# Attention rows scattered straight to expert order, K and V of the dense steps in quarters, logits in 64-column tiles

## The chip, the cores and the metric

The kernel runs on one core of a Trainium2 chip. The metric is the device time of one launch in microseconds (us). A profiled execution also has a span, from its first to its last instruction.

## What is computed

Sparse attention over 4 batches, 8 heads, 768 positions and 64 numbers a head, and then a layer of 8 experts of which each of the 3072 tokens uses one:

```python
scores = scale * np.matmul(q, k.transpose(0, 1, 3, 2))
mask = np.abs(blk_i - blk_j) <= 1                  # blocks of 32
mask |= (blk_i == 0) | (blk_j == 0) | (blk_i == 23) | (blk_j == 23)
# and three sampled key blocks for every query block
attn = softmax(np.where(mask, scores, -1e9)); x = attn @ v
x = x.transpose(0, 2, 1, 3).reshape(3072, 512)
logits = x @ w_gate; e_idx = argmax(logits)
gate_w = softmax(logits)[e_idx]; eom = sigmoid(x @ w_output_gate)
for e in range(8):
    m = e_idx == e
    out[m] = gate_w[m] * eom[m, e] * (np.maximum(x[m] @ w1[e], 0) @ w2[e])
```

## The kernel before

**Attention** runs in 52 steps, 26 for each of two batch pairs (`bp`). The first four of a pair are dense (the first and last query block see all keys; `u` numbers the step, each takes two heads of both batches), the other 22 are sparse: 11 pairs of query blocks (`i`), each in two steps (`hg`). A step's stages are spread over three turns of the loop at L1125: turn n computes scores of unit n (`pS`, L454 and L523), the O product of unit n-2 (`pO`, L488 and L554) and the transposes of unit n-1 (`pT`). Around them `at(step, rank, f, ...)` hangs loads, copies and routing (L970 to L1055). The order of each engine's instructions is the order of the program (`in_order`, L80), and a load that is `paced` (L93) waits for the last TensorE instruction ahead of it.

K of a batch pair is one tile `kn`, 3.1 MB, V of the dense steps one tile `vn`, 3.1 MB; the first pair loads them at the start (L980 to L984), K in two halves and then V in six parts; the second pair's come in twelve loads at steps 8 to 24 (L999 to L1001). For a sparse pair the kernel copies K blocks into a ring `kr` on GpSimd (`gather_k`, L384, and `fixed`) and VectorE (`window_k`, L401), and gathers V rows from device memory with two indirect DMAs on GpSimd's queue (`gather_v`, L411), 128 rows of 4160 B each, into a ring `vt` of three.

**Routing.** Each 128 finished tokens (a tile, 24 in all) go to device memory as `xscr` (`store_x`, L578, two stores on SyncE's queue), are transposed (`turn`, L585), and give 16 logits by four fp32 matmuls (`route_p`, L603), which the trace shows as eight passes. In groups of tiles (`RG`, L45) VectorE works out expert, gate and the place of each token in expert order (`route_a`, L614, and `route_c`, L661); `route_d` (L695) scatters rows of 16 B (output index, row in `xscr`, gate) into the DRAM tensor `table`. `plan_ops` (L712) then makes the list of expert units: units 0 and 1 are tiles of experts 0 and 1 that are started before routing ends; 15 further ones (and a conditional rest) are single tiles or pairs.

**Expert part.** `program` (L1062) lays it out in steps, eight to a unit, one for each 128 of the 1024 hidden numbers. For unit u, whose first step is t = 8u: `load_t` (t-18) fetches its part of the table on SyncE's queue, `load_x` (t-9) gathers its x rows by it on GpSimd's queue, `x_s` (t-7) splits x in two halves of fp16 (ScalarE, VectorE), `x_t` (t-5) transposes it, for units from 4 on by DMA transposes on SyncE's queue. `piece_load` (L1059) loads the 512 KB weight pieces on SyncE's queue into a ring of 16, only when the expert changes; `w_h` and `w_l` split them (ScalarE, VectorE); `p_h` and `p_y` are the matmuls, `h_h` and `h_l` the ReLU halves `hh`; `y_o` scales, `store_y` (t+13) writes by an indirect DMA on GpSimd's queue; the second store of a pair waits for the first to land. The buffers of `tab` are four: `load_t` of unit u needs that of u-4, which `store_y` frees. The plan stands at step 6 (`PLAN`, L63).

The lines on which steps of the prediction rest:

```python
src = table[ds(row[0], 128 * m)].rearrange("(p m) c -> p m c", m=m)   # L814, load_t
after_scatters(nc.sync.dma_start(tabs[u][:, 0:m], src).ins)
nc.gpsimd.indirect_dma_start(                                         # L841, load_x
    xfs[u][:, m], None, src, bass.IndirectOffsetOnAxis(ap=tabs[u][:, m, 1:2], axis=0))
nc.tensor.matmul(lp[:, 0:16], x[:, c], wst[:, c], start=c == 0, stop=c == 3)   # L607
```

Of the kernel before, what the change touches and what calls it, by code (L numbers as in the profile page):

```python
# [27 lines left out]
NROW = EMPTY + 1024  # L28

# [15 lines left out]
RG = ((0, 4), (4, 8), (8, 12), (12, 16), (16, 19), (19, 24))  # L45
GT = max(b - a for a, b in RG)

GE = 3
# [14 lines left out]
PLAN = 6, (40,)  # L63
# [9 lines left out]
PARTS = (5, 5, 4), (5, 5)  # L73
# [35 lines left out]
def tile_kernel(ctx, tc, q, k, v, sampled, wg, wcat, out):  # L109
# [15 lines left out]
    xscr = dram.tile([NTOK, DM], F32, name="xscr")  # L125

    table = dram.tile([NROW, 4], I32, name="table")

# [15 lines left out]
    lim = const.tile([1, NE], F32, name="lim")  # L144
    base8 = const.tile([128, 8], F16, name="base8")
    tile8 = const.tile([PS, 8], I32, name="tile8")
    tilef = const.tile([PS, 8], F32, name="tilef")
    vals = const.tile([128, NT, 4], I32, name="vals")
# [36 lines left out]
    wi = sp.tile([128, NPAIR, 2], I32, name="wi")  # L185
    wf = sp.tile([128, NPAIR, 2], F32, name="wf")
    dup = sp.tile([128, NB, 3], F32, name="dup")

    def setup_iota():
# [13 lines left out]
        nc.gpsimd.iota(vals[:, :, 1], pattern=[[128, NT]], base=0, channel_multiplier=1)  # L203
        nc.gpsimd.memset(vals[:, :, 3], 0)
# [16 lines left out]
    def setup_const():  # L221
# [8 lines left out]
        nc.vector.tensor_scalar(lim, iota128[0:1, 0:NE], float(LS), 128.0, op0=ALU.mult, op1=ALU.add)  # L230

# [6 lines left out]
    def setup_vals():  # L238
# [5 lines left out]

        nc.gpsimd.memset(places, 0)
# [21 lines left out]
    def setup_index():  # L267
# [19 lines left out]
        nc.vector.tensor_copy(vals[:, :, 0], vf.rearrange("p a b -> p (a b)"))  # L287
# [41 lines left out]
    def setup_rest():  # L329

        tz = stg.tile([128, 1024], F32, tag="stg", name="tz").bitcast(I32)[:, 0:NROW // 32].rearrange("p (n c) -> p n c", c=4)
        nc.gpsimd.memset(tz, 0)
        nc.gpsimd.memset(tz[:, :, 0:1], 2 * NTOK)
        nc.sync.dma_start(table.rearrange("(p n) c -> p n c", p=128), tz)


    ntt = NT
# [6 lines left out]
    kr = [ring.tile([128, 12, 256], F32, name=f"kr{i}") for i in range(RK)]  # L344
# [4 lines left out]
    kn, vn = {}, {}  # L349

    def prep_alloc(bp):
        kn[bp] = big.tile([128, NB, 256], F32, tag="kn", name=f"kn{bp}", bufs=2)

    def prep_alloc_v(bp):
        vn[bp] = big.tile([128, 6, 2, 8, VW], F32, tag="vn", name=f"vn{bp}", bufs=1)

    def load_k(bp, c):
        nc.sync.dma_start(kn[bp][:, c], k[bp, :, c])

    def load_v(bp, c):  # L360
        nc.sync.dma_start(vn[bp][:, c].rearrange("p b j w -> p (b j w)"), v[769 * bp + 128 * c:769 * bp + 128 * c + 128])
# [10 lines left out]

    def fixed(bp, r):
        for j in range(2):
            nc.gpsimd.tensor_tensor(
                kr[r][:, 10 + j], kn[bp][:, 23 * j], eighth.to_broadcast([128, 256]), op=ALU.mult)
# [7 lines left out]
    def gather_k(bp, i, kind, ns):  # L384
# [5 lines left out]
        for n, rv in zip(ns, regs):  # L390
            slot = n + 4 if n < 3 else n - 2
            if kind == "dve":
                nc.vector.tensor_single_scalar(r[:, slot:slot + 1], kn[bp][:, ds(rv, 1)], EXPS, op=ALU.mult)
            elif kind == "act":
                nc.scalar.activation(r[:, slot:slot + 1], kn[bp][:, ds(rv, 1)], AF.Copy, scale=EXPS)
            else:
                nc.gpsimd.tensor_tensor(  # L397
                    r[:, slot], kn[bp][:, ds(rv, 1)].rearrange("p o n -> p (o n)"), eighth.to_broadcast([128, 256]),
                    op=ALU.mult)

    def window_k(bp, i):  # L401
        a = 1 + 2 * i
        r = kr[i % RK]
        nc.vector.tensor_single_scalar(r[:, 0], kn[bp][:, a + 2], EXPS, op=ALU.mult)
        nc.vector.tensor_single_scalar(r[:, 7:10], kn[bp][:, a - 1:a + 2], EXPS, op=ALU.mult)
# [13 lines left out]
    xt = {}  # L419

    def new_x(bp, i):
        if (bp, i) not in xt:
            xt[bp, i] = att.tile([128, 2, 4, D], F32, tag="x", name=f"x{bp}_{i}", bufs=3)
        return xt[bp, i]
# [787 lines left out]
```

## Time and profile before

| | |
|---|---|
| median of three runs | 628.8 us (625.73 to 629.6) |
| profiled execution | 631.68 us |
| its span | 629.9 us |
| its mean granted TensorE clock | 0.951 |
| busy share of the span: TensorE, its weight loads, VectorE, ScalarE, GpSimd | 88%, 62%, 63%, 53%, 37% |

A line of a timeline has start and length in us, the engine, the source line, operation, output and inputs, the count of merged instructions, and in brackets the idle time before it and what ended it. PE is TensorE, PEld its weight loads, DVE VectorE, ACT ScalarE, POOL GpSimd, SPq the queue of SyncE. A wait is put down to what came last by the profile and can be another one.

### The profile page before, as it was taken

Reading aid. Unit: us, or ns where it says so; the run is one execution under the profiler, and the core shown is the slowest. Engines: PE = TensorE matmul, PEld = TensorE weight load, DVE = VectorE, ACT = ScalarE, POOL = GpSimd, SP = SyncE. Lnnn points to the kernel's source line nnn. Section 1 sums busy time; section 2 is a strip of 40 time slices with the busy share of each in tenths; the row PEclk is TensorE's granted clock in tenths of the full one; section 3 lists DMA queues with packets and bytes.
Section 4 is the critical chain, followed back from the end, with each engine's and each line's share of the span. In section 5 each row is a group of like instructions: output and inputs, shape, how many; then the busy total and the mean of one; then the engine's idle time right before and its main releaser. Section 6 shows DMA issues by size and latency. Waiting matters only on the chain. (4 is left out here: it accounts for less than half of the span.)

```text
span 629.9 us, 18639 instructions
## 1 busy us (share of the span) xinstructions
PE 553.2 (88%) x7234; PEld 390.7 (62%) x7234; DVE 396.1 (63%) x741; ACT 335.2 (53%) x584; POOL 230.6 (37%) x317
## 2 busy tenths in 40 slices
PE   4788998798898899878699987999969999799993
PEld 3366776575676676656466655666646666566662
DVE  3468676554684666847967575656656566585560
ACT  1445565455465456555467574555744556465550
POOL 4256666736266656541421203122122203222021
PEclk7698999989999999899799999999988999899997
DMA  8747999984599998664294299962947617667962
GB/s 316 212 106 219 284 304 276 240 242 80 136 237 317 291 288 242 136 185 107 79 400 164 71 284 303 333 154 52 271 147 221 187 34 252 168 201 225 298 247 105
DMA packets 68796, 132.53 MB, mean 210 GB/s; under 512 B 32479, under 2 KB 38751, under 8 KB 68448
## 3 DMA queue, kind: packets, MB, share of 16 engines
q1 hardware_dynamic: 56960, 93.65, 49.3%
q0 software_dynamic: 11744, 37.64, 20.6%
q8 instruction: 59, 0.97, 0.6%
q14 instruction: 33, 0.27, 0.1%
HBM read 137.58 MB, written 14.12 MB: 241 GB/s over the span
## 5 line engine op out<-in xcount | busy, mean ns | idle before, releaser
L910 PEld LDWEIGHTS <-kr 128*128 128x128 f16 x1200 | 105.7, 100 | 52.6 <-issue 22.8
L895 DVE SCALAR_TENSOR_TENSOR kr<-r,kr 128x1024 f16<-128x1024 f32 (+1 forms) x104 | 119.9, 1179 | 23.5 <-ACT kr L891 18.5
L910 PE MATMUL h<-xb,kr 128*128 128x256 f16 (+1 forms) x1080 | 121.3, 263 | 13.7 <-DVE hh L925 7.1
L941 PE MATMUL y<-kr,hh 128*128 128x512 f16 x501 | 127.3, 385 | 0.0
L955 POOL DMA_INDIRECT out_dram<-yo,tab x28 | 32.7, 1168 | 237.7 <-ACT yo L949 181.1
L891 ACT ACTIVATE kr<-r 128x1024 f16<-128x1024 f32 (+1 forms) x104 | 102.4, 1018 | 0.8 <-DMA r<-in_wcat_dram 0.5
L941 PEld LDWEIGHTS <-hh 128*128 128x128 f16 x672 | 64.9, 99 | 52.2 <-issue 3.0
L397 POOL TENSOR_TENSOR kr<-kn,eighth 128x256 f32<-128x256 f32 x132 | 77.8, 618 | 16.2 <-issue 15.9
L919 ACT ACTIVATE hh<-h 128x512 f16<-128x512 f32 (+1 forms) x68 | 35.2, 518 | 89.6 <-PE h L910 85.3
L414 POOL DMA_INDIRECT vt<-in_v_dram,vidx x44 | 43.6, 992 | 82.6 <-PE O L508 41.9
L472 DVE TENSOR_REDUCE mx<-S 128x4 f32<-128x1024 f32 x44 | 53.7, 1221 | 28.6 <-PE S L465 20.5
L480 ACT ACTIVATE P<-S,mx 128x256 f32<-128x256 f32 x176 | 69.5, 488 | 3.1 <-DVE mx L472 2.3
L925 DVE SCALAR_TENSOR_TENSOR hh<-h,hh 128x512 f16<-128x512 f32 (+1 forms) x68 | 40.4, 594 | 48.7 <-ACT hh L919 48.7
L433 ACT COPY pt<-T 128x512 f32<-128x512 f32 x66 | 37.0, 590 | 43.1 <-PE T L430 36.1
L465 PE MATMUL S<-kr,qall 64*32 64x256 f32 x1408 | 53.0, 402 | 1.0 <-issue 0.8
L895 DVE SCALAR_TENSOR_TENSOR ws<-r,ws 128x1024 f16<-128x1024 f32 (+1 forms) x39 | 44.1, 1146 | 14.6 <-ACT ws L891 14.6
L430 PE MATMUL T<-ident,P 128*128 128x128 f32 x352 | 50.4, 289 | 0.1
L508 PE MATMUL O<-vt,pt 128*32 128x65 f32 x1408 | 34.4, 225 | 12.9 <-DMA vt<-in_v_dram,vidx 11.0
L910 PEld LDWEIGHTS <-ws 128*128 128x128 f16 x432 | 35.8, 98 | 14.0 <-ACT kr L891 2.4
L941 PE MATMUL y<-ws,hh 128*128 128x512 f16 x171 | 43.8, 388 | 0.0
L430 PEld LDWEIGHTS T<-ident,P 128*128 128x128 f32 x352 | 41.7, 148 | 2.4 <-issue 0.4
L910 PE MATMUL h<-xb,ws 128*128 128x256 f16 (+1 forms) x360 | 38.4, 256 | 3.4 <-DMA xb<-xb 1.9
(233 smaller groups left out, 689.9 us busy)
## 6 DMA issues: line engine op xcount, KB each, us to landing
r<-in_wcat_dram SPq DMA_DIRECT2D x152, 512.0 KB
vn<-in_v_dram SPq DMA_DIRECT2D x12, 520.0 KB
qall<-in_q_dram SPq DMA_DIRECT2D x24, 256.0 KB
xscr<-x SPq DMA_DIRECT2D x48, 128.0 KB
vc<-in_v_dram SPq DMA_DIRECT2D x22, 260.0 KB
kn<-in_k_dram SPq DMA_DIRECT2D x2, 1536.0 KB
kn<-in_k_dram SPq DMA_DIRECT2D x6, 512.0 KB
vc<-in_v_dram SPq DMA_DIRECT2D x12, 130.0 KB
```

The lines of the kernel that those rows point to most:

```text
L397: nc.gpsimd.tensor_tensor(r[:, slot], kn[bp][:, ds(rv, 1)].rearrange("p o n -> p (o n)"), eighth.to_broadcast([128, 256]), op=ALU.mult)
L414: nc.gpsimd.indirect_dma_start(vt[bp, i][:, s].rearrange("p b j w -> p (b j w)"), None, v, bass.IndirectOffsetOnAxis(ap=vidx[:, bp, i, s:s ...
L430: nc.tensor.transpose(pt[:, 128 * c:128 * c + 128], p[:, 128 * c:128 * c + 128], ident)
L433: nc.scalar.copy(t[:, 0:w], pt[:, 0:w])
L465: nc.tensor.matmul(s[64 * h2 + 32 * qi:64 * h2 + 32 * qi + 32, b, hp], t[p, 64 * j + 32 * qi:64 * j + 32 * qi + 32], g[p, 1 - qi:3:1 + qi, ...
L472: nc.vector.tensor_reduce(mx, self.s.rearrange("p b h n -> p (b h) n"), axis=AX.X, op=ALU.max, negate=True)
L480: nc.scalar.activation(p[:, 256 * hp:256 * hp + 256], self.s[:, b, hp], AF.Exp, bias=self.mx[:, 2 * b + hp:2 * b + hp + 1])
L891: nc.scalar.activation(w[:, 0, r], piece(n // 8, n % 8)[:, r], AF.Copy, scale=SW)
L895: nc.vector.scalar_tensor_tensor(w[:, 1, r], piece(n // 8, n % 8)[:, r], SW, w[:, 0, r], op0=ALU.mult, op1=ALU.subtract)
L910: nc.tensor.matmul(hps[n // 2][:, cols(n)], w[:, hl, 128 * c:128 * c + 128], x[:, xl, c], start=cnt == 0, stop=cnt == 11)
L925: nc.vector.scalar_tensor_tensor(hl[:, k], hps.pop(g)[:, k], 0.0, hh[:, k], op0=ALU.max, op1=ALU.subtract)
L941: nc.tensor.matmul(y, a[:, k], w[:, l, 512:1024], start=n % 8 == 0 and cnt == 0, stop=n % 8 == 7 and cnt == 2)
```

## The change

K is laid out by dense step (`u`): a quarter of 786 KB each, and `kr`, the score matmuls and the copies take 64-number runs. The halves of an array that held the two batches of a pair now hold two halves of the heads, so that a token's 512 numbers of x lie in one partition. V of the dense steps is a second copy in device memory in the order of the steps, four loads of 799 KB into the ring `vt`; for the second pair they stand at steps 23, 25, 27 and 28. `vn` is gone. `xscr` and `table` are gone: x lies in a ring `xall` of 8 tiles whose rows have 16 more places, for output index and gate; `route_d` scatters these rows of 2112 B to `rows`, in expert order. The first four routing groups have three tiles instead of the first three of four. The plan works out place indices (`place_u`) of each unit's rows, `load_x` gathers `rows` by them, and `keep_t` copies index and gate out of the gathered rows on GpSimd. `load_t` only reads registers. Ten weight pieces instead of twelve are loaded early, six instead of four at the end of attention.

The core of the diff:

```diff
-RG = ((0, 4), (4, 8), (8, 12), (12, 16), (16, 19), (19, 24))
+RG = ((0, 3), (3, 6), (6, 9), (9, 12), (12, 16), (16, 19), (19, 24))
...
-PLAN = 6, (40,)
+PLAN = 6, (60,)
...
-    def load_k(bp, c):
-        nc.sync.dma_start(kn[bp][:, c], k[bp, :, c])
...
+    def load_k(bp, u, c):
+        nc.sync.dma_start(kn[bp][:, u, c], k[bp, u, :, c])
...
+    def load_v(bp, u):
+        t = ring.tile([128, 2, 2, 8, VW], F32, tag="vt", name=f"vq{bp}_{u}", bufs=RV)
+        t = t.rearrange("p a b j w -> p (a b j w)")[:, 0:VQ]
+        nc.sync.dma_start(t, vdense[4 * bp + u])
...
-    def store_x(bp, i, tt):
-        rows = xscr[128 * tt:128 * tt + 128]
...
+        nc.gpsimd.tensor_copy(x[:, DM:DM + 1], vals[:, tt:tt + 1])
...
         for c in range(4):
-            nc.tensor.matmul(lp[:, 0:16], x[:, c], wst[:, c], start=c == 0, stop=c == 3)
+            for h in range(2):
+                nc.tensor.matmul(
+                    lp[64 * h:64 * h + 64, 0:16], x[:, c, 64 * h:64 * h + 64], wst[:, c], start=c == 0, stop=c == 3)
...
     def route_d(t):
         i = nc.gpsimd.indirect_dma_start(
-            table, bass.IndirectOffsetOnAxis(ap=place[:, t:t + 1], axis=0), vals[:, t], None).ins
+            rows, bass.IndirectOffsetOnAxis(ap=place[:, t:t + 1], axis=0), x_of(t).bitcast(I32), None).ins
...
+        ends = sp.tile([PS, 17], F32, tag="bad", name="ends")
+        yield nc.vector.tensor_copy(ends[:, 0:16].rearrange("p (t e) -> p t e", t=2), cp[0:PS, 0:8].unsqueeze(1).to_broadcast([PS, 2, 8]))
+        yield nc.vector.memset(ends[:, 16:17], 0.0)
+        yield nc.vector.tensor_tensor(ee[:, 1], own[:, 0], ends, op=ALU.mult)
...
+        lb = bank("lb", True)
+        nc.tensor.matmul(lb[:, 0:2 * PS], ones[0:PS], left.rearrange("p a b -> p (a b)"), start=True, stop=True)
...
+        yield nc.vector.tensor_single_scalar(place_u[:, NE:], lu, float(EMPTY), op=ALU.add)
...
     def load_t(u):
         m = tiles_of(u)
-        tabs[u] = rt.tile([128, 2, 4], I32, tag="tab", name=f"tab{u}", bufs=4)
...
-        after_scatters(nc.sync.dma_start(tabs[u][:, 0:m], src).ins)
...
+    def keep_t(u):
...
+        nc.gpsimd.tensor_copy(tabs[u][0][:, 0:m], xfs[u][:, :, DM])
+        nc.gpsimd.tensor_copy(tabs[u][1][:, 0:m], xfs[u][:, :, DM + 1])
...
-            nc.gpsimd.indirect_dma_start(
-                xfs[u][:, m], None, src, bass.IndirectOffsetOnAxis(ap=tabs[u][:, m, 1:2], axis=0))
+            after_scatters(nc.gpsimd.indirect_dma_start(
+                xfs[u][:, m].bitcast(I32), None, rows, bass.IndirectOffsetOnAxis(ap=place_u[:, u, m:m + 1], axis=0)).ins)
...
-    load_k(0, slice(0, 12))
-    load_k(0, slice(12, 24))
-    scale_q(0, NPAIR)
-    for c in range(6):
-        load_v(0, c)
+    for u in range(3):
+        load_k(0, u, slice(0, NB))
+        load_v(0, u)
+        if u == 0:
+            scale_q(0, NPAIR)
+    load_k(0, 3, slice(0, NB))
...
+    at(2, 1, load_v, 0, 3)
...
-    for c in range(6):
-        at(8 + 3 * c, 3, load_k, 1, slice(4 * c, 4 * c + 4))
-        at(9 + 3 * c, 3, load_v, 1, c)
+    for c in range(8):
+        at(8 + 2 * c, 3, load_k, 1, c // 2, slice(12 * (c % 2), 12 * (c % 2) + 12))
+    for u in range(4):
+        at(PER + (-3, -1, 1, 2)[u], 1, load_v, 1, u)
...
-            at(r, 3, store_x, bp, i, tt)
...
-    for j in range(8 * NE):
-        at((PER + ND + 1 + j, PER + ND + 1 + j, NSTEP - 3 + (j - 12))[j // 6], 3, prefetch_w, j)
+    for j in range(NRAW):
+        at(PER + ND + 1 + j if j < NRAW - 6 else NSTEP - 3 + (j - NRAW + 6), 3, prefetch_w, j)
...
+            do(t + 1, 13, keep_t, u)
```

## Rows read from the trace of the kernel before

**Rows 1.** The page: the span in 40 slices of 15.75 us.

```profile
PEclk7698999989999999899799999999988999899997
DMA  8747999984599998664294299962947617667962
GB/s 316 212 106 219 284 304 276 240 242 80 136 237 317 291 288 242 136 185 107 79 400 164 71 284 303 333 154 52 271 147 221 187 34 252 168 201 225 298 247 105
```

**Rows 2.** Waits: engine, line waited for; us in total, times, longest.

```profile
PE h L910 <- DVE hh L925: 13.3, 4, 4.7
...
PE O L508 <- DMA vt<-in_v_dram,vidx: 11.0, 9, 2.6
...
PE h L910 <- DMA xb<-xb: 7.2, 3, 2.9
```

**Rows 3.** Timeline of the first 16 us, VectorE and TensorE.

```profile
10.22 0.47 DVE L327 CAST vidx<-tab 128x22 int32<-128x22 f32 x1
...
13.73 0.90 PE L532 MATMUL S0d<-kn,qall 64*64 64x384 f32 x1 [2.14 <-DMA kn<-in_k_dram]
...
15.34 0.96 DVE L540 TENSOR_REDUCE mx0d<-S0d 128x1 f32<-128x768 f32 x1 [4.65 <-PE S1d L532]
```

**Rows 4.** Timeline of TensorE in a sparse step with logits.

```profile
88.58 1.09 PE L465 MATMUL S<-kr,qall 64*32 64x256 f32 x32
89.61 1.06 PE L607 MATMUL lp<-wst,xT 128*128 128x16 f32 x8
90.60 0.69 PE L497 MATMUL O<-vc,pt 128*64 128x65 f32 x16
91.22 0.67 PE L508 MATMUL O<-vt,pt 128*32 128x65 f32 x32
...
92.83 1.09 PE L465 MATMUL S<-kr,qall 64*32 64x256 f32 x32
```

**Rows 5.** The page: DMA issues, count and KB of each.

```profile
r<-in_wcat_dram SPq DMA_DIRECT2D x152, 512.0 KB
vn<-in_v_dram SPq DMA_DIRECT2D x12, 520.0 KB
...
xscr<-x SPq DMA_DIRECT2D x48, 128.0 KB
...
kn<-in_k_dram SPq DMA_DIRECT2D x6, 512.0 KB
```

**Rows 6.** Timeline: a V gather on GpSimd's queue, and TensorE.

```profile
95.88 0.97 POOL L414 DMA_INDIRECT vt<-in_v_dram,vidx  x1 [0.52 <-PE O L508]
...
104.88 0.66 PE L508 MATMUL O<-vt,pt 128*32 128x65 f32 x30 [1.72 <-DMA vt<-in_v_dram,vidx]
```

**Rows 7.** Waits of SyncE's queue.

```profile
SPq L815 <- DMA out_dram<-yo,tab: 55.3, 9, 8.0
...
SPq L806 <- DMA table<-vals,place: 9.6, 2, 5.7
```

**Rows 8.** Timeline of GpSimd late in attention: the first x gather.

```profile
268.88 0.98 POOL L841 DMA_INDIRECT xf<-xscr,tab  x1 [5.75 <-DMA vc<-in_v_dram]
270.16 1.43 POOL L414 DMA_INDIRECT vt<-in_v_dram,vidx  x1 [0.30 <-issue]
```

**Rows 9.** Timeline of the plan: VectorE's first and last instruction, and TensorE.

```profile
299.86 0.15 DVE L717 TENSOR_SCALAR ci<-cp 19x8 int32<-19x8 f32 x1
...
305.07 0.14 DVE L773 CAST es<-most 19x1 int32<-19x1 f32 x1
...
306.85 1.44 PE L910 MATMUL h<-xs,kr 128*128 128x128 f16 x12 [4.73 <-DVE hh L925]
```

**Rows 10.** Timeline of one round of expert units.

```profile
441.50 9.21 SPq L820 DMA_DIRECT2D r<-in_wcat_dram  x6
...
450.80 4.43 SPq L865 DMA_TRANSPOSE xb<-xb  x2
...
458.65 1.47 PE L910 MATMUL h<-xb,ws 128*128 128x256 f16 x12 [1.91 <-DMA xb<-xb]
...
466.26 1.06 ACT L851 ACTIVATE xb<-xb 128x1024 f16<-128x1024 f32 x1 [8.21 <-issue]
...
470.36 2.72 PE L910 MATMUL h<-xb,kr 128*128 128x256 f16 x12 [3.72 <-DVE hh L925]
```

More of the change, by code (lines that the diff above doesn't have):

```diff
@@ L27 @@
 EMPTY = E * LS
-NROW = EMPTY + 1024
+NROW = EMPTY + 1
+XP = DM + 16
+VQ = 6 * 2 * 2 * 65
+VGAT = 2 * (S + 1)
+NX = 8
+NRAW = 16
+OOB = 4096
 NE = 2
@@ L122, in tile_kernel @@
     psO = actx.enter_context(tc.tile_pool(name="psO", bufs=2, space=PSUM))
-    xscr = dram.tile([NTOK, DM], F32, name="xscr")
-    table = dram.tile([NROW, 4], I32, name="table")
+    rows = dram.tile([NROW, XP], I32, name="rows")
     ident = const.tile([128, 128], F32, name="ident")
@@ L144, in tile_kernel @@
     lim = const.tile([1, NE], F32, name="lim")
+    early = const.tile([128, NE], F32, name="early")
+    rowid = const.tile([128, PS, 2], F32, name="rowid")
+    place_u = const.tile([128, NE + PS, 2], I32, name="place_u")
     base8 = const.tile([128, 8], F16, name="base8")
@@ L230, in setup_const @@
         nc.vector.tensor_scalar(lim, iota128[0:1, 0:NE], float(LS), 128.0, op0=ALU.mult, op1=ALU.add)
+        nc.vector.tensor_scalar(early, iota128[:, 0:NE], float(LS), pcol[:, 0:1], op0=ALU.mult, op1=ALU.add)
+        nc.vector.tensor_copy(rowid, rid)
         nc.vector.tensor_scalar(tri, iota128, pcol[:, 0:1], None, op0=ALU.is_gt)
@@ L329, in setup_rest @@
     def setup_rest():
[L331 to L337, printed above, removed]
+        nc.gpsimd.memset(xall[0:1, NX - 1, 0:DM], 0.0)
+        nc.gpsimd.memset(xall[0:1, NX - 1, DM:DM + 1], float(OOB))
+        nc.sync.dma_start(rows[EMPTY:EMPTY + 1], xall[0:1, NX - 1].bitcast(I32))
     oh = const.tile([128, NT, 8], F16, name="oh")
@@ L527, in pS @@
             for half in range(2):
[L528 to L531 removed]
+                for b in range(2):
+                    for h2 in range(2):
+                        j = 2 * u + b
+                        p = slice(64 * h2, 64 * h2 + 64)
                         nc.tensor.matmul(
[L533 to L534 removed]
+                            self.s[h2][64 * b:64 * b + 64, half, 0:384], t[p, 64 * j:64 * j + 64],
+                            kn[bp][p, u, 12 * half:12 * half + 12, 32 * b:32 * b + 32], start=True, stop=True)
         def dM(self):
@@ L546, in aE @@
                 for half in range(2):
[L547 removed]
+                    p = att.tile([128, XP], F32, tag="P", name=f"P{b}{half}" + self.name, bufs=6)
                     nc.scalar.activation(p[:, 0:384], self.s[b][:, half, 0:384], AF.Exp, bias=self.mx[b])
@@ L668, in route_c @@
             yield nc.vector.scalar_tensor_tensor(c0, lack, 0.0, c0, op0=ALU.max, op1=ALU.add)
+            over = rt.tile([128, NE], F32, name="over")
+            yield nc.vector.tensor_tensor(over, early, rp[:, 256:256 + NE], op=ALU.is_lt)
+            yield nc.vector.scalar_tensor_tensor(over, early, float(-EMPTY), over, op0=ALU.add, op1=ALU.mult)
+            yield nc.vector.tensor_single_scalar(place_u[:, 0:NE, 0], over, float(EMPTY), op=ALU.add)
         t0, t1 = RG[g]
@@ L827, in xring @@
             for i in range(3):
-                t = ring.tile([128, 2, 1024], F32, tag="vt", name=f"xb{i}", bufs=RV)
-                xbuf.extend(t[:, c] for c in range(2))
-        return xbuf[n]
+                t = ring.tile([128, 2 * (DM + XP)], F32, tag="vt", name=f"xb{i}", bufs=RV)
+                xbuf.append(t)
+        return xbuf[n % 2 if n < 4 else 2][:, (slice(0, 2 * XP), slice(2 * XP, 2 * XP + 1024), slice(1024 * (n % 2), 1024 * (n % 2) + 1024))[n // 2]]
     def load_x(u):
@@ L1087, in program @@
             if n >= 8 * NE:
-                do(max(n - 16 - LEAD + 1, end), 14, piece_load, n, n1 + ahead)
+                do(max(n - NRAW - LEAD + 1, end), 14, piece_load, n, n1 + ahead)
+            elif n >= NRAW:
+                do(n - NRAW - LEAD + 1, 14, prefetch_w, n)
             do(PH.get(n, n), 8, p_h, n)
```

232 lines of the change are left out of this document (119 added, 113 removed).

## Prediction

> **What bounds the kernel now.** I read the page's slices first, then the waits, then the timeline of four places: the start, a sparse step, the join of attention and experts, and one round of expert units. The slices [rows 1] are 15.75 us each. The first 18 or so are attention, the rest the expert part; the DMA engines are at 0.9 or more in slices 5 to 8 and 12 to 15, at 237 to 317 GB/s, and in the expert part they swing between 0.1 and 0.9. TensorE (PE) is the engine that the end hangs on. In a sparse step without waits [rows 4] it works without a gap: S at 88.58, logits at 89.61, O at 90.60, the next S at 92.83, so 4.25 us of which the logits hold 0.99. What PE waits for is in [rows 2]: 11.0 us for gathered V in nine waits, 13.3 us on `hh` and 7.2 us on transposed x in the expert part. After a long wait the same work also runs slower: 12 matmuls that took 1.47 us at 458.65 took 2.72 us at 470.36, after 3.72 us idle [rows 10]. So a wait that goes gives back more than its own length.
>
> **The change part by part.** My sum is made against the profiled execution: span 629.9 us, 631.7 us in all. The median of the runs shown, 628.8, is 2.9 lower; I subtract the same saving from both.
>
> *Start.* The first dense step needed all of K (3.1 MB, two loads); its second half let PE start at 13.73, and the first reduction ran at 15.34 [rows 3]. Now it needs a quarter, 786 KB, which is half of the 1.57 MB of the first old load, so it should land near 6 to 7 us. Next in line is VectorE: its setup ends at 10.69 (10.22 plus 0.47 [rows 3]), and the two setup instructions added stand ahead of its wait for the sampled blocks. The reduction then starts at 10.7: 4.6 us earlier. Low end 0, if a later quarter is late (the four quarters of K and three of V go out alternately, 5.5 MB before the last); high end 7, if PE also leaves its slow clock sooner. I take 4.6. The K copies for the first sparse step, on GpSimd (POOL) and VectorE, now wait for the fourth quarter; the four dense steps before that step cover them.
>
> *Logits.* Per tile of 128 tokens, 8 passes with 128 weight columns took 0.99 us (89.61 to 90.60). The new form is 16 passes with 64 columns; the nearest row is the O product, 16 passes of 128*64 in about 0.62 us [rows 4]. So 0.37 us a tile, 24 tiles, 8.9 us at most, and only where PE and not a transfer sets the step. The low end is a loss: twice the passes at the old 0.12 us each, 23.8 us more. It is nearest to the O row, which has the same tile form, so I take the gain, at half the tiles: 4.5 us.
>
> *K and V loads of the second batch pair.* Before, every three steps of the first sparse run brought 512 KB of K and 520 KB of V [rows 5], 0.69 MB for the two steps of a block pair. Now 393 KB of K per pair; V comes as four 799 KB loads around the second dense run, where slice 10 shows the DMA engines at 0.4 [rows 1]. That is 0.3 MB less per pair, 1 us at 290 GB/s, over eight pairs with full queues. The gather at 95.88 needed until 104.88 to serve PE, which lost 1.72 us [rows 6]. Bounds: 0 if gathers stay late, 11.0 [rows 2] plus the slow work behind. I take 5. Two of the twelve early weight pieces (512 KB each [rows 5]) also move to the end of attention; 3.6 us of transfer out of full slices; I take 1 of 0 to 3.6.
>
> *x rows.* The 48 stores of 128 KB [rows 5] go from SyncE's (SP's) queue; 24 scatters of 128 rows x 2112 B (270 KB) replace 24 of 16 B rows in POOL's queue. The count and the issue time on POOL stay, the bytes on the engines too (6.3 against 6.5 MB). Added are one copy of a column per tile and two per unit on POOL; between gathers POOL has idle time before its wait on PE (0.5 us at 95.88 [rows 6]) and that covers them; uncovered, at the 0.15 us of VectorE's shortest instructions [rows 9], 24 of them would be 3.6 us. The K copies read four runs of 64 numbers instead of 256 in a row; the same idle time covers a step's copies unless they grow by 0.5 us together. The V gathers now queue behind scatters: see the second rival. A seventh routing group puts some twenty short VectorE instructions more under PE's steps, nothing on the path.
>
> *No table.* POOL stood 5.75 us at 268.88 before its first x gather, with the V gathers of the last pairs behind it [rows 8]; the profile names a V load, but SP waited 9.6 us twice in all for the scatters of the table before it could fetch it [rows 7], and the gather needs that table. Now the gather waits for its scatters alone, issued a step earlier. I take 2.5 us of 0 to 5.75 for PE. In the expert part SP's table load had to wait for a free table buffer, that is for an old store of the output: 55.3 us in nine waits, up to 8.0 [rows 7], with weight loads behind it in SP's queue. At 441.50 six came in a row, and the transposes of x at 450.80, behind them in the same queue, served PE only at 458.65 (wait 1.91); the store and the x gather came late in turn, ScalarE stood 8.21 us until 466.26, and PE 3.72 us until 470.36 [rows 10]. Without the table, loads start up to 8 us earlier, in time when the DMA engines idle (0.2 and 0.1 in slices 28 and 33 [rows 1]). At stake: 7.2 plus 13.3 less 4.73 (the plan, below), 15.8 us, and some 6 us of slow work behind three such rounds (an estimate: two blocks a round, 1.25 us longer each, 2.72 less 1.47, with a lighter round among them): 0 to 22. The store, not the table, stays ahead of the x gather on POOL, so I take a third: 7.
>
> *Plan.* VectorE's plan ran from 299.86 to 305.21, and PE stood 4.73 us for the `hh` behind it [rows 9]. Eleven short instructions (0.15 us like the rows, plus gaps) and one matmul go in: 2.2 us. The matmul stands in PE's queue right behind the plan's first, so PE now waits before, not after, some 2.7 us of expert work, and does that work once the plan lets it go. Loss between 1.5 and 5; I take 2.5.
>
> Sum: 4.6 + 4.5 + 5 + 1 + 2.5 + 7 - 2.5 = 22.1 us. 631.7 - 22.1 = 609.6 for a profiled execution, 628.8 - 22.1 = 606.7 for the median: **607 us**.
>
> **Rivals.**
> (a) *The expert part gives nothing* (SP's wait was slack: six loads in a row still end before the weights are used, and the x gather stays behind the store): 15.1 us remain, 614. For it: no wait of weight in [rows 2]; against it: the queue order at 450.80.
> (b) *The scatters hold up the V gathers*: slower. Nineteen scatters have a gather queued behind them. At 95.88 a gather of 532 KB took 8 us from its issue's end to PE [rows 6]; a scatter of half the bytes would add up to 4 us, if full. With 2 us each, 38 us: 628.8 + 38 - 22 = 645. It decides from 22.1 / 19 = 1.2 us each. Against it: the same bytes went over the same engines before, and the relief in K and V is as large. The Trainium skill ("DMA: Bandwidth & Descriptors", "Queues, rings and completion order") has each DMA engine take turns between queue rows; by it the gathers and scatters would now share POOL's turn, while SP's queue keeps its own. No row here shows the turns.
> (c) *The narrow logits cost double*, since each moves only 16 columns: 23.8 lost instead of 4.5 won, 628.8 - 17.6 + 23.8 = 635. The Trainium skill ("TensorEngine Tiling (Array Packing)", "Performance Considerations") warns of this: a small matmul has a fixed overhead, so tiling should not be taken from a dimension that is small already. The O row speaks against it: 16 such passes in 0.62 us.
> (d) *Nearly all is given back*: the plan at its worst, the DMA relief nil, the expert part nil: head, half the logits and the table leave 4.6 + 4.5 + 2.5 - 5 = 6.6: 622.
> (e) *More*: MoE waits gone wholly (22) and the relief doubled: 587.
>
> **How the numbers follow.** The forecast, within 10 us of 607, 0.45; (a) 0.15; (d) 0.13, of which half lies within 1% of 628.8; (e) 0.12; (b) 0.10; (c) 0.05. Range 590 to 627: it takes in (a), (d) and part of (e), and leaves out (b), (c) and the extremes, 0.2. About 1% is what a measurement can tell from no change here. Faster by over 1%: 0.45 + 0.15 + 0.12 + half of (d), 0.78; within 1%: 0.08, with a little of (b); slower 0.14.
>
> **What would show it.** First reduction near 10.7 us; logits of 0.6 us; fewer waits of O for V before slice 9; no 5 us stand of POOL before the first x gather; SP without waits on the output's stores, weight loads spread out, and PE's waits on transposed x and `hh` shorter; a longer stand around the plan. I am wrong if V's waits grow, with POOL's scatters in front, or if the expert part keeps its waits though SP's are gone.

## The result, and the profile after

The changed kernel takes 607.6 us, the kernel before 627.3 us on the same chip (medians of four runs each). Ratios, here and below, compare only the faster runs of each kernel: the changed kernel's four took 601.3, 603.3, 612.0 and 612.2 us, and the faster pair gives a ratio of 0.960 (95% interval 0.953 to 0.967), where the medians would give 0.969. The prediction was 607. The profiled executions, 631.7 and 603.3 us, are 28.4 us apart, and all readings below compare these two unless another run is named. The sum came out; its terms did not, and the largest failure is worth nearly as much as the whole change.

This is where the time went. I cut both traces at the same instructions of TensorE: the first S of each sparse run, the first S of the second dense run, the plan's first matmul, and ScalarE's first and last output block (us).

| stretch | before | after | gain |
|---|---|---|---|
| start to first sparse run | 38.78 | 31.99 | 6.8 |
| first sparse run | 103.92 | 89.04 | 14.9 |
| second dense run | 27.27 | 25.99 | 1.3 |
| second sparse run and routing | 129.33 | 121.89 | 7.4 |
| plan to first output | 15.57 | 17.52 | -1.9 |
| first to last output | 305.39 | 306.54 | -1.1 |

The other 1.1 us lie behind the last output block. The 6.8 us of the start belong to this profile: in the eight profiles of variants of the changed kernel the first sparse run begins between 33.8 and 35.5 us, so 3.3 to 5.0 us earlier than before.

The slices of the page of after (15.04 us each) answer to [rows 1]. The granted clock is 0.9 or more from slice 2 to 12:

```profile
PEclk8999999999998997997999998999989999899998
DMA  8856989958889876736923788827548347479791
```

What TensorE waits for (engine, line waited for; us in total, times, longest), against [rows 2]: gathered V fell from 11.0 to 4.2 and transposed x from 7.2 to 0.8, but `hh` grew from 13.3 to 15.0, beside a new wait at the plan. As 4.7 of the 13.3 stood at the plan [rows 9], `hh` grew from 8.6 to 15.0 like for like.

```profile
PE h L945 <- DVE hh L960: 15.0, 4, 6.9
...
PE lb L803 <- DVE left L799: 6.8, 1, 6.8
PE O L521 <- DMA vt<-in_v_dram,vidx: 4.2, 3, 2.5
...
PE h L945 <- DMA xb<-xb: 0.8, 1, 0.8
```

The start, timeline of after, against [rows 3]. The first reduction runs at 10.73 instead of 15.34. VectorE's last setup instruction starts just ahead of it, at 10.64, as forecast, but TensorE's passes of the first dense step start at 7.82 and the last one shown ends at 10.65, so both bound it together.

```profile
7.82 0.87 PE L545 MATMUL S0d<-kn,qall 64*64 64x384 f32 x1 [2.66 <-DMA kn<-in_k_dram]
...
9.81 0.84 PE L545 MATMUL S1d<-kn,qall 64*64 64x384 f32 x1
...
10.64 0.18 DVE L337 CAST vidx<-tab 128x22 int32<-128x22 f32 x1
10.73 0.95 DVE L553 TENSOR_REDUCE mx0d<-S0d 128x1 f32<-128x768 f32 x1
```

A sparse step with logits, TensorE, against [rows 4]. The 16 passes hold 0.49 us (77.86 to 78.35) where 8 held 0.99, and the step is 3.72 instead of 4.25 us.

```profile
76.84 1.09 PE L478 MATMUL S<-kr,qall 64*32 64x256 f32 x32
77.86 0.65 PE L613 MATMUL lp<-wst,xT 128*64 128x16 f32 x16
78.35 0.67 PE L510 MATMUL O<-vc,pt 128*64 128x65 f32 x16
78.95 0.67 PE L521 MATMUL O<-vt,pt 128*32 128x65 f32 x32
79.54 1.09 PE L442 MATMUL T<-ident,P 128*128 128x128 f32 x8
80.56 1.09 PE L478 MATMUL S<-kr,qall 64*32 64x256 f32 x32
```

SyncE's waits, against [rows 7]. The 55.3 us on output stores are gone. Instead the weight loads wait for their own buffers, which VectorE's weight split frees; the row of before for the same wait (L820) is 20.4 us in 24 times.

```profile
SPq L856 <- DVE kr L930: 88.3, 51, 9.0
...
SPq L856 <- DVE ws L930: 39.0, 21, 7.6
```

And one round of expert units, GpSimd, ScalarE and TensorE, against [rows 10]. The second store of a pair stands until 432.43, 6.7 us behind the first. The two gathers of x follow it, ScalarE stands 8.15 us for the first of them, and TensorE 4.16 us, whose next block then takes 1.85 us.

```profile
425.71 1.66 POOL L990 DMA_INDIRECT out_dram<-yo,tab  x1 [10.58 <-ACT yo L984]
432.43 1.85 POOL L990 DMA_INDIRECT out_dram<-yo,tab  x1 [5.07 <-DVE hh L960]
434.58 0.98 POOL L876 DMA_INDIRECT xb<-rows,place_u  x1 [0.30 <-issue]
435.87 0.97 POOL L876 DMA_INDIRECT xb<-rows,place_u  x1 [0.30 <-issue]
```

```profile
439.43 1.06 ACT L886 ACTIVATE xb<-xb 128x1024 f16<-128x1024 f32 x1 [8.15 <-issue]
```

```profile
443.54 1.85 PE L945 MATMUL h<-xb,kr 128*128 128x256 f16 x12 [4.16 <-DVE hh L960]
```

### The profile page after: what moved, and what is told of

It is laid out like the page before. It is cut to its first block, busy times and chain, and to the rows that moved or that the text cites. A ratio compares the mean times of both kernels' runs of the same rounds, so it can differ in the third digit from the quotient of the medians.

```text
span 601.5 us, 18954 instructions
## 1 busy us (share of the span) xinstructions
PE 532.6 (89%) x7421; PEld 376.0 (63%) x7421; DVE 400.2 (67%) x775; ACT 334.4 (56%) x586; POOL 246.4 (41%) x376
## 5 line engine op out<-in xcount | busy, mean ns | idle before, releaser
L945 PE MATMUL h<-xb,kr 128*128 128x256 f16 (+1 forms) x1080 | 119.7, 261 | 13.8 <-DVE hh L960 11.2
L976 PE MATMUL y<-kr,hh 128*128 128x512 f16 x501 | 125.6, 382 | 0.0
L410 POOL TENSOR_TENSOR kr<-kn,eighth 128x256 f32<-128x256 f32 x132 | 79.1, 627 | 7.7 <-issue 6.1
L930 DVE SCALAR_TENSOR_TENSOR ws<-r,ws 128x1024 f16<-128x1024 f32 (+1 forms) x39 | 43.8, 1139 | 15.6 <-ACT ws L926 15.6
L478 PE MATMUL S<-kr,qall 64*32 64x256 f32 x1408 | 51.2, 394 | 0.9 <-issue 0.9
L945 PE MATMUL h<-xb,ws 128*128 128x256 f16 (+1 forms) x360 | 39.7, 261 | 5.5 <-DVE hh L960 3.8
L876 POOL DMA_INDIRECT xb<-rows,place_u x28 | 34.7, 1241 | 11.4 <-issue 8.2
```

The source lines that it names most:

```text
L410: nc.gpsimd.tensor_tensor(r[:, slot], kn[bp][:, :, ds(rv, 1)].rearrange("p u o n -> p u (o n)"), e8th, op=ALU.mult)
L478: nc.tensor.matmul(s[64 * b + 32 * qi:64 * b + 32 * qi + 32, h2, hp], t[p, 64 * j + 32 * qi:64 * j + 32 * qi + 32], g[p, 1 - qi:3:1 + qi, ...
L930: nc.vector.scalar_tensor_tensor(w[:, 1, r], piece(n // 8, n % 8)[:, r], SW, w[:, 0, r], op0=ALU.mult, op1=ALU.subtract)
L945: nc.tensor.matmul(hps[n // 2][:, cols(n)], w[:, hl, 128 * c:128 * c + 128], x[:, xl, c], start=cnt == 0, stop=cnt == 11)
L976: nc.tensor.matmul(y, a[:, k], w[:, l, 512:1024], start=n % 8 == 0 and cnt == 0, stop=n % 8 == 7 and cnt == 2)
```

## The experiments

The experiments fall into four groups, in the order of running not of telling, and the kernel before ran beside each. Its median there was 634.3, 632.8, 629.9 and 629.8 us, so times of different groups are compared by their ratio to it. Stretches are cut as in the table above.

### Logits alone, logits undone, V loads late

The narrow logits alone, in the kernel before:

```
-            nc.tensor.matmul(lp[:, 0:16], x[:, c], wst[:, c], start=c == 0, stop=c == 3)
+            for h in range(2):
+                nc.tensor.matmul(
+                    lp[64 * h:64 * h + 64, 0:16], x[:, c, 64 * h:64 * h + 64], wst[:, c], start=c == 0, stop=c == 3)
```

> The kernel before with one part of the change alone: logits in 16 passes with 64 token columns instead of 8 with 128. The traces give 0.99 us a tile before (89.61 to 90.60) and 0.49 us after (77.86 to 78.35), so 0.50 us, 12.0 us for 24 tiles where TensorE sets the step. Theory A (the logits carry most of the gain in attention): 12 us less than before, about 615. Theory B (in the first sparse run late transfers set the step, so that only the second run gains): 6 us less, about 621. My rival of twice the cost per tile: 24 us more, 651.

Measured: 627.7 us, ratio 0.993 (0.989 to 0.998), 4.3 us less. In size that is nearer to theory B's 6 us than to theory A's 12, but its place speaks against B: the first sparse run is 100.1 us, 3.9 less, and the rest of attention, by this one profile, brought nothing, as the plan starts at 299.4 us where it started at 299.3 before.

The opposite edit in the changed kernel:

> The changed kernel with the logits put back to 8 passes of 128 token columns. Here transfers are no longer late in the first sparse run, so both theories expect the full 0.50 us for 24 tiles: 12 us more than the changed kernel, about 618 to 620; 9 us more or less would say that the step has slack of its own behind the logits (one of the five groups that follow waits for something else anyway).

Measured: 620.7 us, ratio 0.981 (0.972 to 0.990) where the changed kernel has 0.960, so 13 us more, with an uncertainty of some 7 in both together. The traces say less: the plan starts at 280.5 us. In five profiles of kernels whose attention is that of the changed kernel (268.9, 274.5, 276.9, 275.9 and 273.3) it starts at 273.9 on average, so some 6.6 us are logits in attention. The five lie 8 us apart, so one profile tells this to a few us only. The rest of the difference lies in the expert part, which the edit doesn't touch. I take 4 to 7 us for the logits.

The late V loads, in the kernel before:

```
-        at(9 + 3 * c, 3, load_v, 1, c)
+        at(PER - 6 + c, 1, load_v, 1, c)
```

> The kernel before with the six V loads of the second pair of batches (520 KB each) moved from steps 9, 12, 15, 18, 21, 24 to steps 20 to 25, so that most of the first sparse run has only K loads beside its gathers. Theory B (relief of transfers is the larger part of the 14.9 us that the first sparse run gained: 5.5 us of those are logits, 9.4 are left): 7 to 9 us less than before, about 619, with the gain in the first sparse run and fewer waits of O for V there. Theory A (the logits carry it, and gathers that come late are late for another reason): within 2 us of before, 625 to 629. Six loads close together may cost the end of that run up to 4 us.

Measured: 632.0 us, ratio 0.998 (0.993 to 1.003): no gain. Both edits together:

> The kernel before with both: narrow logits and the late V loads. If the two gains only add up, this gives the sum of the two single runs. Theory B says more than the sum: with gathers in time the narrow logits gain in the first run too (12 us in all) and TensorE keeps its clock; 19 to 22 us less than before, about 607. Theory A: 12 us less, 615.

Measured: 629.0 us, ratio 1.000 (0.994 to 1.005), the first sparse run 100.2 us. No synergy: theory B in this form falls. But the edit was a poor test, since all six loads still fall into the same run, only later.

### What is left of the first sparse run

With narrow logits the first run still takes 100.1 us, where the changed kernel takes 91.0 on average. With wide logits in the changed kernel it takes 93.9, where the kernel before takes 103.9. So something else is worth 9 to 10 us. Three candidates were tried. The first, on top of narrow logits and late V loads, is the rest of the load schedule, and the clearing of the table:

```
...
-    for c in range(6):
-        at(8 + 3 * c, 3, load_k, 1, slice(4 * c, 4 * c + 4))
-        at(9 + 3 * c, 3, load_v, 1, c)
+    for c in range(8):
+        at(8 + 2 * c, 3, load_k, 1, slice(3 * c, 3 * c + 3))
+    for c in range(6):
+        at(PER - 6 + c, 1, load_v, 1, c)
...
-    at(6, 3, setup_rest)
+    at(1, 3, setup_rest)
```

> The kernel before with narrow logits, late V loads, the K loads of the second pair in eight pieces of 384 KB at the steps of the changed kernel instead of six of 512 KB, and the clearing of the table (two fills on GpSimd of 1.35 us) at step 1 instead of step 6. With the first two alone the first sparse run took 100.2 us, in the changed kernel it takes 89.0 to 92.1, with the old stores of x added 93.3. Theory K (the pieces of K and the clearing of the table make what is left): first run 92 to 95, 620 or less in all. Theory X (it is the stores of x in SyncE's queue together with the loads, or something that stays): 98 or more; the clearing alone should give 2 us, seen as no wait of 2.3 us on ScalarE near 55 us.

Measured: 618.6 us, ratio 0.988 (0.981 to 0.996); the first run 99.2 us, so by its own bound this is theory X. Step by step the verdict is finer. From the first to the 17th of VectorE's reductions of S, 16 steps, the kernel before needs 72.9 us, with narrow logits 68.9, with late V too 68.9, this one 66.5, and the five of the changed attention 65.4 to 67.1. So over the first 16 of 21 steps nothing is left to explain, and the loss is in the last five: 28.9 us here, 19.9 to 22.3 in the five profiles. The six V loads now crowd together there, and TensorE waits 4.52 us for a gather. But with narrow logits alone, where these loads are spread, the last five steps take 27.4 us as well, so crowding is not the cause of most of it.

```profile
130.60 1.09 PE L508 MATMUL O<-vt,pt 128*32 128x65 f32 x30 [4.52 <-DMA vt<-in_v_dram,vidx]
```

The clearing of the table is seen in VectorE's timeline at the step where it was: before (first fence), a cast of 128x2 numbers takes 1.55 us, and TensorE's S of 50.96 gets its reduction at 52.84. Meanwhile GpSimd fills the table (second fence). With the fills at step 1 the same cast takes 0.17 us (third fence, this experiment). The second, third and fourth step between reductions, 15.2 us together with narrow logits alone (8.1, 2.8, 4.3), shrink to 12.7 (7.1, 2.5, 3.1), all ahead of this run's first load of the second pair's K at 60.07 us.

```profile
50.19 1.55 DVE L280 CAST pf<-pb 128x2 f32<-128x2 int32 x1
...
52.84 1.22 DVE L472 TENSOR_REDUCE mx<-S 128x4 f32<-128x1024 f32 x1
```

```profile
50.87 0.84 POOL L332 MEMSET tz<- 128x864 int32 x1
51.77 0.50 POOL L333 MEMSET tz<- 128x216 int32 x1
```

```profile
50.24 0.17 DVE L280 CAST pf<-pb 128x2 f32<-128x2 int32 x1
```

The second candidate, the old stores of x, added to the changed kernel on SyncE's queue:

```
+    def store_x(tt):
+        to = xscr[128 * tt:128 * tt + 128]
+        x = x_of(tt)[:, 0:DM].rearrange("p (b c) -> p b c", b=2)
+        for h2 in range(2):
+            nc.sync.dma_start(
+                to[:, 256 * h2:256 * h2 + 256].rearrange("(b p) c -> p b c", p=64), x[64 * h2:64 * h2 + 64])
...
+            at(r, 3, store_x, tt)
```

> The changed kernel with the old 48 stores of x (128 KB each, from SyncE's queue, at the old steps) added back beside the scatters, into a tensor that nothing reads. It moves as many bytes more as the run with doubled scatters, through the other queue. After the runs with narrow logits and late V loads, 10 us of the 14.9 us that the first sparse run gained have no cause yet (93.9 us with wide logits against 103.9). Theory S (the stores of x in SyncE's queue, whose wait for VectorE stands ahead of the loads, and whose traffic makes gathers late, are that cause): 10 us or more above the changed kernel, 618 to 628, the first sparse run back near 98, and several us more than with doubled scatters. Theory O (the cause is elsewhere, in the K loads or in VectorE's work): the same as with doubled scatters, 608 to 614.

Measured: 622.4 us, ratio 0.980 (0.973 to 0.988), 2% above the changed kernel's. The first run is 93.3 us against 91.0 on average (89.0 to 92.1 in the five), so theory S fails for that run: 2.3 us. Over all of attention it is not small: the plan starts at 283.5 instead of 273.9, and the total lies in theory S's range and outside theory O's.

The third, the bytes of V, added as six loads into a spare tile:

```
+    spare = big.tile([128, 4, 1024], F32, tag="r", name="spare", bufs=1)
+
+    def load_spare(c):
+        to = spare.rearrange("p a n -> p (a n)")[:, VROW * (c % 3):VROW * (c % 3 + 1)]
+        nc.sync.dma_start(to, v[769 + 128 * c:769 + 128 * c + 128])
...
+    for c in range(6):
+        at(9 + 3 * c, 3, load_spare, c)
...
```

> The changed kernel with the six old V loads of 520 KB added back at their old steps 9, 12, 15, 18, 21 and 24, into a spare tile that nothing reads; the quarters stay. The first sparse run then moves 25.6 MB like before (26.3) instead of 22.4. Late V loads in the kernel before didn't test this: all six still fell into the same run. Theory V (the 3.1 MB of V that the change takes out of the first run are what is left of its gain): first run 97 to 100 us instead of 89 to 92, at 255 to 263 GB/s, with waits of O for gathered V and a granted clock below 1.00 in it; 614 to 620 in all. Theory N (bytes in that run don't count, as the 2.6 MB of the added stores of x at 268 GB/s cost it only 1 to 2 us): 91 to 93, under 611 in all; the cause then lies in what VectorE and GpSimd do.

Measured: 610.0 us, ratio 0.970 (0.961 to 0.979); the first run 92.9 us, 1.9 above the average. Theory V falls too, though TensorE's waits for V come back in that run (3.9 us in four). Its plan starts at 271.0 us, 2.9 earlier than the average of the five. Busy times and rates of the first run, one row each (the length, then busy times of TensorE, its weight loads, VectorE, ScalarE and GpSimd, TensorE's granted clock, the DMA engines' share, GB/s) for before, after, the added stores and the added loads:

```profile
38.78:142.70 103.92, 94.98 (x2096) 72.77 (x2096) 69.69 (x176) 55.07 (x132) 63.52 (x105) 0.95 0.87 253
```

```profile
31.99:121.03 89.04, 85.80 (x2167) 64.75 (x2166) 72.51 (x189) 55.13 (x133) 70.04 (x122) 1.00 0.81 250
```

```profile
35.27:128.55 93.28, 86.72 (x2167) 65.60 (x2166) 69.53 (x189) 55.06 (x133) 70.04 (x122) 1.00 0.87 268
```

```profile
35.48:128.40 92.92, 86.63 (x2167) 66.26 (x2166) 70.82 (x189) 55.02 (x133) 69.51 (x122) 0.98 0.85 269
```

The rows say what the single runs can't. The changed kernel carries either load again at 268 and 269 GB/s with TensorE's clock at 0.98 to 1.00, and before, at 253 GB/s and 0.95, TensorE was busy 9.2 us longer with the same attention and idle 5.7 us longer. Of the 9.2, 5.0 are the wide logits, since with them the changed kernel is busy 90.8 us there. The four single prices, logits 3.9, clearing 2.5, stores 2.3, V 1.9, make 10.6 of the 12.9 us between 103.9 and the average 91.0. The other 2.3 weren't isolated, and no run put back the routing groups or the old layout of K. Each price comes from one profile: the stores' and V's lie only 1.2 and 0.9 us above the longest of the five. That the parts cost more together, because work behind a long wait runs slower (2.72 us instead of 1.47 in [rows 10], where the granted clock is 0.51 from 469 to 475 us and 1.00 from 458 to 464), fits the rows but was not tried.

### The price of a scatter

```
...
+        i2 = nc.gpsimd.indirect_dma_start(
+            rows2, bass.IndirectOffsetOnAxis(ap=place[:, t:t + 1], axis=0), x_of(t).bitcast(I32), None).ins
...
```

> The changed kernel with every scatter of x rows issued twice, the second into a DRAM tensor that nothing reads: 24 more instructions of 1.05 us on GpSimd and 6.5 MB more, all in GpSimd's queue ahead of gathered V. My rival of scatters that hold up the gathers, at its own price of 2 us each for the 19 with a gather behind them: 38 us more than the changed kernel, 646; from 1.2 us each, 23 us, it would have turned the change. The theory that a scatter fits between two gathers: GpSimd is busy 70 of 89 us in the first sparse run and takes another 11 us there without a stall of TensorE: under 6 us more, 608 to 614.

Measured: 631.7 us, ratio 0.998 (0.994 to 1.002): the second scatters cost as much as the whole change brings, some 24 us, and the first run takes 99.8 us. My "under 6" fell. GpSimd's timeline shows how. In the changed kernel (first fence) the step shown, with a scatter, leaves GpSimd no idle time beyond the gaps between instructions: from gather to gather 4.26 us, where TensorE needs 3.72. With two scatters (second fence) it is 5.65.

```profile
88.04 0.98 POOL L427 DMA_INDIRECT vt<-in_v_dram,vidx  x1 [0.31 <-PE T L442]
89.05 1.75 POOL L410 TENSOR_TENSOR kr<-kn,eighth 128x256 f32<-128x256 f32 x3
90.96 1.03 POOL L712 DMA_INDIRECT rows<-xall,place  x1 [0.16 <-issue]
92.30 0.98 POOL L427 DMA_INDIRECT vt<-in_v_dram,vidx  x1 [0.30 <-PE T L442]
```

```profile
97.47 0.98 POOL L428 DMA_INDIRECT vt<-in_v_dram,vidx  x1 [0.30 <-issue]
98.45 0.20 POOL L599 COPY xall<-vals 128x1 f32<-128x1 f32 x1
98.60 1.75 POOL L411 TENSOR_TENSOR kr<-kn,eighth 128x256 f32<-128x256 f32 x3
100.51 1.03 POOL L713 DMA_INDIRECT rows<-xall,place  x1 [0.17 <-issue]
101.85 0.97 POOL L716 DMA_INDIRECT rows<-xall,place  x1 [0.30 <-issue]
103.12 0.99 POOL L428 DMA_INDIRECT vt<-in_v_dram,vidx  x1 [0.30 <-issue]
```

So in these steps the price is GpSimd's own time to issue, 1.3 us with its gaps. What the 270 KB add was not separated: up to the plan's start the second scatters cost 17.4 us, and as many bytes in stores from SyncE's queue 9.6. The kernel before paid the time to issue too, for rows of 16 bytes (24 scatters of 1.01 us, the median). That is why rival (b) did not come true, although a scatter is about as dear as the 1.2 us from which it decided.

### The expert part

Output stores no longer ordered among each other:

```
-            nc.gpsimd.indirect_dma_start(
+            i = nc.gpsimd.indirect_dma_start(
                 out, bass.IndirectOffsetOnAxis(ap=tab[:, m:m + 1], axis=0), t, None,
-                bounds_check=NTOK - 1, oob_is_err=False)
+                bounds_check=NTOK - 1, oob_is_err=False).ins
+            tc.declare_no_dep(i, group="outs", reason="tokens differ")
+            tc.add_to_no_dep_group("outs", i)
```

> The changed kernel with the output stores no longer ordered among each other (the tokens of two stores differ). In the expert part the second store of a pair stood 6.7 us on GpSimd until the first had landed (425.71 to 432.43), the gathers of x behind it went at 434.58 and 435.87, ScalarE stood 8.15 us until 439.43 and TensorE 4.16 us until 443.54. Theory W (that order is what makes x late): the gathers go 5 to 7 us earlier, TensorE's waits of 14.8 us on `hh` shrink to under 4 and the slow work behind them goes too: 12 to 18 us less than the changed kernel, 590 to 596. Theory L (x waits for transfers of weights or for SyncE's queue, whatever its issue time): within 3 us of the changed kernel.

Measured: 594.7 us, ratio 0.941 (0.933 to 0.950). The gather of x earlier instead:

```
-                do(max(t - 9, end + 1), 1, load_x, u, n1 + min(ahead, 1))
+                do(max(t - 12, end + 1), 1, load_x, u, n1 + min(ahead, 1))
```

> The changed kernel with the gather of x for a unit issued three steps earlier, and so ahead of the store of the unit before the last in GpSimd's queue; the stores stay as they are, with the second of a pair behind the first. Theory W (x is late only because it stands behind the store): 12 to 18 us less than the changed kernel, 590 to 596, like the run with unordered stores. Theory L: within 3 us. If this gains and the run with unordered stores doesn't, the time from issue to landing is the cause, not the store.

Measured: 587.1 us, ratio 0.926 (0.919 to 0.933), 20 us less than the changed kernel. Theory W holds in its direction in both, but not in its sizes: with unordered stores the wait on `hh` fell to 7.1 us and not under 4, and the early gather brought more than the 12 to 18 us. The 6.7 us between the two stores of a pair were their order, although the profile named `hh`. Without it they go 1.3 us apart:

```profile
427.61 1.02 POOL L990 DMA_INDIRECT out_dram<-yo,tab  x1 [11.29 <-ACT yo L984]
428.94 2.04 POOL L990 DMA_INDIRECT out_dram<-yo,tab  x1 [0.30 <-ACT ws L926]
```

The expert part from first to last output, for after, unordered stores and early gather, one row each with the columns of above. Under the two experiments stands what TensorE waited for longest there:

```profile
286.40:593.00 306.60, 287.25 (x2151) 193.99 (x2148) 191.65 (x199) 174.14 (x225) 71.18 (x83) 0.98 0.65 207
```

```profile
292.40:584.80 292.40, 283.40 (x2151) 192.79 (x2148) 191.84 (x199) 174.59 (x225) 80.78 (x83) 0.99 0.68 216
```

```profile
PE h L945 <- DVE hh L960: 7.1, 3, 4.3
```

```profile
294.50:577.00 282.50, 281.27 (x2151) 192.28 (x2148) 192.40 (x200) 175.39 (x224) 79.79 (x81) 1.00 0.74 224
```

```profile
PE h L945 <- DVE xb L909: 0.9, 1, 0.9
```

With the early gather TensorE stands 1.2 us in 282.5. The gain is in three places: between ScalarE's output blocks the changed kernel needs 21.4, 19.4 and 18.1 us in the stretches of the three units with a single tile, with unordered stores 17.9, 16.0 and 15.2, with the early gather 13.1, 13.1 and 13.5. Such a unit gives TensorE 13 us of work, and the way of x (store, landing, second store, gather, split, transpose) is longer than that.

That x was late behind the store was in the profile of before [rows 10], and I named it ("the store, not the table, stays ahead of the x gather on POOL"). GpSimd's rows of that round, before:

```profile
459.11 1.95 POOL L955 DMA_INDIRECT out_dram<-yo,tab  x1 [5.27 <-DMA xb<-xb]
461.37 0.99 POOL L841 DMA_INDIRECT xb<-xscr,tab  x1 [0.30 <-issue]
```

The table's removal did not touch it. On the chip of the first group, the expert part is 302.4 and 301.1 us in two profiles that still have the table, and 311.9 with wide logits in the changed kernel. Over all profiles it is 301.1 to 305.4 with the table (four) and 306.5 to 312.5 without (five, stores and gather as in the change). So taking the table out did not shorten this part: it is 1.1 us longer between the two profiles, some 8 us by the averages. TensorE's wait on transposed x fell, from between 3.8 and 7.2 to between 0.8 and 2.8, and its wait on `hh` rose, from between 6.8 and 11.9 to between 15.0 and 19.2. What trades the one for the other was not isolated.

### The plan, and the best version

Both edits of the expert part together, and the plan in two parts, so that a step of expert work stands between TensorE's two matmuls:

```
-PLAN = 6, (60,)
+PLAN = 6, (38, 22)
```

> The changed kernel with the early gather of x, the unordered stores, and the plan in two parts, so that a step of expert work stands between TensorE's two matmuls of the plan. Expert part 282 us like the run with the early gather, the last store about 1.3 us earlier, and from the plan's first matmul to the first output 15.5 us instead of 17.6, if the second matmul's place is what the plan cost; 17.5 again, if VectorE's longer row of instructions is. 583 to 586 in all.

Measured: 583.0 us, ratio 0.928 (0.922 to 0.935); the plan to the first output 17.4 us. In three parts (20, 18, 22):

> As the run before it, with the plan in three parts, the first two of VectorE's 38 instructions ahead of the second matmul. VectorE then serves `hh` between the parts: from the plan's first matmul to the first output 13 to 15 us, 581 to 584 in all. If x for the third unit comes too late because the plan ends two steps later, a wait of TensorE on x near 300 us takes it back.

Measured: 584.1 us, ratio 0.933 (0.926 to 0.940); the plan 17.1 us. In six profiles with the plan in one part it is 17.2 to 17.9 (and 20.7 with doubled scatters, left aside), so the place of the matmul is worth under 0.5 us. Of the two branches for two parts the second came true, VectorE's longer row at 17.5 us; the 13 to 15 us for three parts did not. In two parts TensorE does 1.3 us of work more ahead of the matmul and then stands 5.56 us for the same row of VectorE's instructions.

```profile
282.96 0.19 PE L803 MATMUL lb<-left,ones 19*128 19x38 f16 x1 [5.56 <-DVE left L799]
```

These two and the early gather alone lie within each other's intervals. All beat the changed kernel by over 2.5% and the kernel before by about 7%. Splitting the plan and freeing the stores add nothing that was measured beside the early gather.

## Why the prediction was right, and where it was not

*Start, 4.6 us:* right. 15.34 to 10.73 is 4.61; the bound named next (VectorE's setup, 10.69) was there, its last instruction starting at 10.64, with TensorE's passes beside it. At the first sparse run 4.4 us of it are left on average of the five profiles.

*Logits, 4.5 us of at most 8.9:* right in sum, with two errors in it. The tile costs 0.49, not 0.62 us, so 12.0 were there to be had; 4 to 7 came. As I read it, in steps with a scatter GpSimd's 4.26 us, and before the change late transfers, set the step. Half of what was possible was a guess that held. Rival (c) is refuted, by sign. The overhead of small matmuls behind the Trainium skill's warning ("TensorEngine Tiling (Array Packing)", "Performance Considerations") does not show here: twice the matmuls, each with half the tile, took half the time. The Trainium skill warns of splitting a dimension that is small already, and here the 128 columns were split, not the 16.

*K and V of the second pair, 5 us:* mis-sized. Putting the V loads back costs 1.9 us in that run, and the early weight pieces and the K pieces were not separated. The waits for V fell as predicted (11.0 to 4.2), but with narrow logits alone they fell to 6.6, so only part of that can be the loads'.

*x rows, 0 us:* this step failed. I let the bytes cancel (6.3 against 6.5 MB) and costed the stores' place in SyncE's queue at nothing. Put back, they cost 2.3 us in the first run and 9.6 us by the plan. That idle time of GpSimd covers the added work failed too: in the step with a scatter shown above none is left.

*No table, 2.5 us:* the stand of 5.75 us at the first x gather [rows 8] is gone (after, 0.15 us at 236.28, below). What that gave TensorE was not measured by itself. What I overlooked is the clearing of the table: two fills that held up VectorE under TensorE's S, 2.5 us.

```profile
236.28 1.35 POOL L876 DMA_INDIRECT xf<-rows,place_u  x1 [0.15 <-issue]
```

*Expert part, 7 us:* this step failed; it is rival (a). My own sign of being wrong came true: the part kept its waits though the SyncE waits of 55.3 us [rows 7] went. Nothing came of those, since the weight loads now wait 88.3 us for buffers instead. I had read a long wait of a queue as a loss without asking whether the queue had slack. The 20 us at stake were there, and one line (the step at which x is gathered) takes them.

*Plan, -2.5 us:* right: 17.2 to 17.9 against 14.7 to 15.6 in four profiles with the table, 2.3 us on average. The 2.2 us that I put down to the longer row of instructions are borne out. That the matmul's place in TensorE's queue adds to them is not: moving it brought under 0.5 us.

So attention gave 30.4 us between the two profiles, 25.4 by the average of five, where the sum had 17.6; the expert part took 1 to 8 where it had given 7. The two errors cancelled, and the forecast landed on 607 for reasons that were half its own; that the median, which lies between two pairs of runs, met it so closely is luck. Put together from the runs, attention's 25 us are 4.6 start, 4 to 7 logits, 2.5 clearing, 9.6 stores of x and 1.9 V loads, 23 to 26. This sum mixes prices in the first run (clearing, V) with prices up to the plan (stores), each from one profile, while the five profiles lie 8 us apart. It shows that the parts together are of the right size, not each of them.

## What to carry to other kernels

Before a queue's long wait is booked as a gain, look at what the freed instructions would wait for next, and follow the late consumer back by itself: here the chain store, second store, gather of x was visible, and moving the gather three steps earlier was worth nearly as much as the whole change. An experiment that only shifts a load inside the same stretch does not test whether the load counts. And a sum that lands on the number says nothing about its terms until each has been cut out of the trace.

## What the runs showed of the hardware

- Sixteen fp32 passes with 64 weight columns took half as long as eight with 128, though one load of 64 is not half as long as one of 128: 138 ns against 192 (first two rows: shortest, median and longest load in ns, before and after). In the tile at 77.86 the loads for the two halves start some 7 ns apart and the next pair 57 ns later, where before a load of 128 starts every 111 ns. So two loads of 64 overlap, and eight pairs hold 0.55 us where eight single loads held 0.97 (last two rows).

```profile
L607 PEld LDWEIGHTS lp<-wst,xT x192: 186/192/287, 52.0 to 293.8; 128*128 128x128 f32 x192
L613 PEld LDWEIGHTS lp<-wst,xT x384: 132/138/228, 45.2 to 263.4; 128*64 128x64 f32 x192
89.60 0.97 PEld L607 LDWEIGHTS lp<-wst,xT 128*128 128x128 f32 x8 [0.41 <-ACT pt L433]
77.86 0.55 PEld L613 LDWEIGHTS lp<-wst,xT 128*64 128x64 f32 x16 [0.41 <-ACT pt L445]
```

- A VectorE cast of two numbers per partition took 1.55 us beside GpSimd's fill and 0.17 us without it. The Trainium skill ("SBUF — State Buffer", "SBUF: two separate sides") has VectorE in some forms and GpSimd share a port pair that one of them holds for a whole instruction. The rows agree in direction: the cast ends at 51.74, the longer fill at 51.71. They don't show the lock itself, as the cast starts at 50.19 and that fill only at 50.87.
- An indirect store of 128 rows costs GpSimd 1.0 us and a gap of 0.3 whether its rows are 16 or 2112 bytes. In the first run the second scatters cost 8.8 us, and as many bytes more from SyncE's queue 2.3 us; up to the plan 17.4 and 9.6 us.
